# A fused attention and two-layer FFN kernel on one Trainium2 core: attention begun after 11 of 36 bias groups, with four more changes of order

## The chip, the core and the metric

The kernel runs on one core of a Trainium2 chip. The metric is the time of one execution in microseconds (us); the kernel before has a median of 1082.48 us over three runs (1082.42 to 1085.07). The engines are called PE (TensorE, with PEld for its weight loads), DVE (VectorE), ACT (ScalarE), POOL (GpSimd) and SP (SyncE, which here only issues DMAs). All program times below are read from one profiled execution.

## What is computed

Attention over 4 batches, 8 heads, 576 positions of 64 values, with a bias that a small net computes from the distance of two positions; then two FFNs over the 2304 tokens. The parts of the reference that matter:

```python
scores = scale * np.matmul(q, k.transpose(0, 1, 3, 2))
x = (psi_rel / psi_i)[..., None]            # from the positions alone
h = np.maximum(x @ w1 + b1, 0.0)            # 32 hidden values per pair of positions
scores = scores + (h @ w2).transpose(2, 0, 1)[None]
attn = np.exp(scores - np.max(scores, axis=-1, keepdims=True))
attn = attn / (np.sum(attn, axis=-1, keepdims=True) + 1e-09)
x = np.matmul(attn, v)                      # then (2304, 512)
...
h = x @ w_in                                # 512 to 2048, then a rational function g(h)
x = g @ w_out
...
h = np.maximum(np.maximum(x @ w1, x @ w2), x @ w3)   # 512 to 768, three times
out = h @ w_out
```

Weights come in as 64-bit floats; q, k, v and the bias net as 32-bit floats.

## The kernel before

**Bias.** The bias depends on neither batch nor on q and k, so it is made once, in 36 groups of 16 query rows: eight groups for each of the query tiles t = 0 to 3 (128 rows) and four for t = 4 (64 rows). For each group, `bias_hidden` makes four hidden blocks of 128 partitions x 576 columns, the first on ACT (L173), three on DVE (L176); `bias_out` multiplies them with the second layer on PE (L185, 16 records a group), evacuates and scales on ACT (L194, three of the 36 on DVE, L192), and stores the group to a DRAM tensor `bias_d[t]` from ACT's DMA queue (L197). When a tile's last group is stored, `bias_load` fetches that tile's bias for the head pairs p = 0 and 1 back through SP's queue (L204, and L210 to L212 for t = 4); for p = 2 and 3 this comes four units before use. `bias_step` makes the hidden blocks of one group and the output of the group before it.

**Attention.** The work is cut into 80 units (batch b, query tile t, head pair p). In batch 0 the pairs 0 and 1 run first, tile by tile (units 0 to 9: two units for each t); the other pairs run their five tiles one after the other, grouped as ts = [0, 1] and [2, 3, 4]. `attn_tick(n)` does, in the order of a list of step names (`A1` for the first ticks, `A2` for the rest): scores of unit n on PE (`sc`, L233, L243), bias, scale and row minimum on DVE (`r0`, `r1`, L258), exponent and row sum on ACT (`e0`, `e1`, L264), the reciprocal of unit n-1's sums (`n`: POOL L269, DVE L270, POOL L272 spreads it to 128 columns, `rb`), the transposes of unit n-2 (`T`: eight L296, one tail block L302, and the spread reciprocals L303, the last two into one PSUM tile `tt`), their evacuations (`v0` on ACT, `v1` on DVE or ACT), attention x V of a whole group ts (`av`, L338), its scaling by the reciprocals and its store (`st`, L344, L346). The groups of two and three units are cut over as many ticks (`CUT2`, `CUT3`). The step `b` calls `bias_step`; in the first list there are four of it.

**Splits.** q and k are each split into a rounded part and a remainder for PE's fast fp32 form. `split_kq` makes this in six pieces for a head pair, all on POOL (L138 to L153).

**Weights.** The 64-bit weights of the first FFN layer (16 blocks) are converted during attention (`early`: ACT L382, DVE L383 and L391, store to DRAM `wi_n`), spread evenly over the units from `WS` to `WE` by `early_pop` (steps `p1`, `p2`). From unit 61 on they are read back and split (`weight_stages`, ACT L407, remainder L408 on the engine that `low_eng` gives).

**Order.** `manual_schedule` makes the named engines follow the order of the program text; the others get their order from a planner. Before, SP alone follows the text until unit 8; from unit 8 to the end of attention SP, PE and DVE do; five drain ticks behind it run with the first FFN steps in the planner's order; after them all five engines follow the text. The 24 first bias groups stand in the text between the pieces of the first two head pairs' splits (`SB`: two behind each piece), ahead of unit 0.

**Buffers.** 35 slots of SBUF of one size (`slot`) hold hidden blocks, bias outputs, bias tiles, q, k, v, their splits and the exponents. PSUM has two `wide` buffers (bias outputs and scores) and four `bank` buffers (transposes, `tt`, attention x V).

Of the kernel before, what the change touches and what calls it, by code (L numbers as in the profile page):

```python
# [17 lines left out]
P = 128  # L18
# [11 lines left out]
KN = {'NSLOT': 35, 'NRAW': 3, 'NRAWX': 2, 'NATT': 4, 'HB': 0, 'NE': 'd', 'FP': 2, 'BL': 4, 'T4': 0, 'LSP': 1, 'KX': 4, 'HT': 'ss', 'EVP': 'da', 'TTP': 'dda', 'NXS': 4, 'EARLY': 0, 'NM0': 8, 'MAN': 2, 'MANF': 3, 'A1': ['b', 'T', 'sc', 'st', 'r0', 'av', 'b', 'b', 'b', 'sq', 'n', 'r1', 'p2', 'v0', 'v1', 'e0', 'e1'], 'A2': ['sc', 'av', 'p1', 'T', 'r1', 'r0', 'n', 'st', 'p2', 'sq', 'e0', 'e1', 'v0', 'v1'], 'LL': 10, 'SL': 4, 'LL0': 9, 'SL0': 4, 'SQ': [2, 1, 1], 'CUT2': 2, 'CUT3': 3, 'WS': 9, 'WE': 70, 'WT': 61, 'XT': 8, 'XA': 3, 'XB': 8, 'F': ['g2a', 'g2d', 'h', 'g1a', 'w', 'g2p', 'g1d', 'g1p', 'y', 'x', 'g3'], 'LOW': 4, 'LOM': 3, 'LOI': 0, 'GHI': 'dve', 'GLO': 'dve', 'BED': 8, 'BE0': 16, 'NU1': 'pool', 'XE': ['act', 'pool'], 'WR': 1, 'YSP': 'act', 'LAG': 2, 'EV1': 'dve', 'XSE': 'act', 'STQ': 'sp', 'PUQ': 'sp', 'NB0': 0, 'HP': 0, 'SB': 2, 'XLA': 3, 'XLB': 6, 'XSA': 11, 'YL': 10, 'YS': 14, 'WLOW': 1}  # L30
# [7 lines left out]
def tile_attention_moe(  # L38
# [90 lines left out]
    def split_kq(b, p):  # L129
# [4 lines left out]
        lo_eng = pool  # L134
        low = slice(64, P)

        def q_hi():
            pool.tensor_scalar(qs, qr[:, :, :512], 1.0, 0.0, ALU.mult, ALU.add)  # L138

        def q_lo(u):  # L140
            lo_eng.tensor_tensor(qs[low, u], qr[low, u, :512], f32(qs[low, u]), ALU.subtract)

        def k_hi(u):
            pool.tensor_scalar(ks[u][:, 0], kr[:, u], 1.0, 0.0, ALU.mult, ALU.add)

        def k_lo(u):
            pool.tensor_tensor(ks[u][:, 1], kr[:, u], f32(ks[u][:, 0]), ALU.subtract)
# [13 lines left out]
    hid = {}  # L161

    def bias_hidden(t, g):
        hs = []
        for c in range(4):
# [14 lines left out]
    def bias_out(t, g):  # L180
# [106 lines left out]
    def transposes(b, t, p):  # L287
# [315 lines left out]
    bnext = [0]  # L603

    def bias_step():
        i = bnext[0]
        if i < len(bgroups):
            if i == 0:
                bias_hidden(*bgroups[0])
            if i + 1 < len(bgroups):  # L610
                bias_hidden(*bgroups[i + 1])
            t, g = bgroups[i]
# [28 lines left out]
    load_kq(0, 1)
    for p in range(2, KN["FP"]):
        if p == 2:
            load_v(0, 2)
        load_kq(0, p)
    for p in range(KN["FP"]):
        for n, f_ in enumerate(split_kq(0, p)):
            if p >= 2 and KN["LSP"]:
                sqq.append(f_)
            else:  # L650
# [63 lines left out]
    def attn_tick(n):  # L714
# [72 lines left out]
    for n in range(KN["NM0"]):  # L787
        attn_tick(n)
# [101 lines left out]
```

## Time and profile before

| | us |
|---|---|
| median of three runs | 1082.48 (1082.42 to 1085.07) |
| the profiled execution | 1085.02 |
| its span, first to last instruction | 1083.2 |
| PE busy | 1034.7 (96%) |
| DVE busy | 657.7 (61%) |
| ACT busy | 622.8 (57%) |
| POOL busy | 452.7 (42%) |

Engines work side by side, so their busy times don't add up. The stages by the timeline of PE: bias alone from 6 to 59 us, bias and attention to about 88, attention to about 363, the first FFN to about 780, the second to the end. The profile's page cuts the span into 40 equal slices of 27 us; a digit there is the busy share in tenths. In a timeline, each line has the start, the duration, engine, source line, operation, output<-input, shape and count; the bracket behind it is the time in which the engine sat idle before, and what ended it.

### The profile page before, as it was taken

To read this page: it belongs to the slowest core of one execution; us is meant where nothing else is said; L and a number is where in the kernel's file an instruction comes from. 1 tells how busy PE (TensorE), PEld (TensorE's weight loads), DVE (VectorE), ACT (ScalarE), POOL (GpSimd) and SP (SyncE) were. 2 spreads that over 40 slices of the span, in tenths; PEclk is the share of its full clock that TensorE was granted. 3 is DMA by queue.
4 is the path that set the end of the run, shared out by engine and by line. 5 is a ranking of instruction groups with operands and counts; after the bars stand their busy time and mean duration, and the time that the engine had idled before them with its cause. 6 is when DMAs were issued, how large, how long until landed. Compare 5 with 4: busy or idle time off the path is not lost. (4 is left out here: it accounts for less than half of the span.)

```text
span 1083.2 us, 16519 instructions
## 1 busy us (share of the span) xinstructions
PE 1034.7 (96%) x5996; PEld 814.2 (75%) x5996; DVE 657.7 (61%) x1296; ACT 622.8 (57%) x1226; POOL 452.7 (42%) x569
## 2 busy tenths in 40 slices
PE   5689899999998889999999999999999999999998
PEld 2247777777765668878889888788888888888887
DVE  8485667676665789777779877799954211111111
ACT  5685676776776878676678766788733211211111
POOL 7605767677696534332233322333533330211111
PEclk9799999999998889999999999999999999999999
DMA  7486854454453442010020200034243200201010
GB/s 266 138 298 216 294 182 151 158 190 158 157 184 123 147 142 78 1 59 1 0 79 1 79 1 0 24 114 136 84 142 105 78 1 1 78 1 59 1 40 20
DMA packets 43394, 107.94 MB, mean 100 GB/s; under 512 B 4784, under 2 KB 11184, under 8 KB 43312
## 3 DMA queue, kind: packets, MB, share of 16 engines
q1 hardware_dynamic: 38128, 96.27, 26.8%
q10 hardware_dynamic: 5184, 10.62, 2.5%
q8 instruction: 47, 0.77, 0.3%
q14 instruction: 35, 0.29, 0.1%
HBM read 77.90 MB, written 28.97 MB: 99 GB/s over the span
## 5 line engine op out<-in xcount | busy, mean ns | idle before, releaser
L454 PE MATMUL p<-ys,wm 128*128 128x512 f32 (+1 forms) x1080 | 227.0, 368 | 0.0
L454 PE MATMUL ph<-xs,wwi 128*128 128x512 f32 (+1 forms) x960 | 215.9, 373 | 3.5 <-ACT at L743 2.6
L454 PEld LDWEIGHTS p<-ys,wm 128*128 128x128 f32 x1080 | 188.9, 188 | 34.3
L454 PE MATMUL y<-gs,wwo 128*128 128x512 f32 (+1 forms) x905 | 204.4, 373 | 1.3 <-POOL gs L502 1.1
L454 PEld LDWEIGHTS ph<-xs,wwi 128*128 128x128 f32 x960 | 169.7, 190 | 38.4 <-POOL xs L446 3.0
L502 POOL TENSOR_TENSOR gs<-g,gs 128x512 fp32r<-128x512 f32 (+1 forms) x80 | 96.1, 1201 | 237.2 <-ACT gs L501 170.2
L454 PEld LDWEIGHTS y<-gs,wwo 128*128 128x128 f32 x905 | 158.4, 188 | 34.5 <-POOL gs L502 2.4
L264 ACT ACTIVATE e<-e,st 128x576 f32<-128x576 f32 x144 | 111.1, 772 | 61.2 <-DVE st L258 44.3
L258 DVE CUSTOM_DVE_ANT_0 e<-s,bias 128x576 f32<-128x576 f32 x144 | 104.3, 754 | 44.9 <-PE s L233 32.4
L546 POOL TENSOR_TENSOR h2s<-mx,h2s 128x512 fp32r<-128x512 f32 (+1 forms) x30 | 35.5, 1183 | 225.5 <-ACT h2s L545 225.5
L542 DVE TENSOR_TENSOR mx<-p,mx 128x512 f32<-128x512 f32 (+1 forms) x30 | 19.1, 637 | 141.4 <-PE p L454 137.5
L475 ACT ACTIVATE s<-ph,keep 128x512 f32<-128x512 f32 (+1 forms) x80 | 49.5, 618 | 90.3 <-PE ph L454 89.9
L545 ACT CAST h2s<-mx 128x512 fp32r<-128x512 f32 (+1 forms) x30 | 17.3, 578 | 127.8 <-DVE mx L543 127.8
L296 PEld LDWEIGHTS tp<-ident,e 128*128 128x128 f32 x576 | 62.1, 141 | 35.7 <-issue 20.1
L233 PE MATMUL s<-k,qs 128*128 128x288 f32 x512 | 86.4, 309 | 2.2 <-ACT bo L194 1.5
L296 PE MATMUL tp<-ident,e 128*128 128x128 f32 x576 | 81.5, 281 | 1.2 <-ACT at L743 1.2
L477 DVE SCALAR_TENSOR_TENSOR g<-g,keep,s 128x512 f32<-128x512 f32 (+1 forms) x80 | 55.3, 692 | 41.5 <-ACT g L476 40.4
L338 PE MATMUL av<-at,v 128*64 128x320 f32 (+3 forms) x576 | 79.0, 396 | 0.0
L560 PE MATMUL o<-wmo,h2s 128*128 128x512 f32 x324 | 78.6, 390 | 0.0
L233 PEld LDWEIGHTS s<-k,qs 128*128 128x128 f32 x512 | 71.3, 191 | 5.6 <-issue 2.6
L185 PE MATMUL pb<-h,keep 128*32 128x288 f32 x576 | 49.2, 450 | 24.1 <-ACT h L173 23.2
L560 PEld LDWEIGHTS o<-wmo,h2s 128*128 128x128 f32 x324 | 60.4, 188 | 12.6 <-POOL h2s L546 0.4
(98 smaller groups left out, 1599.6 us busy)
## 6 DMA issues: line engine op xcount, KB each, us to landing
bias_d<-bo ACTq DMA_DIRECT2D x36, 288.0 KB, 3.1
kr<-in_k SPq DMA_DIRECT2D x16, 576.0 KB, 4.3
qr<-in_q SPq DMA_DIRECT2D x16, 576.0 KB, 4.3
bias<-bias_d SPq DMA_DIRECT2D x16, 576.0 KB, 5.5
wrm<-in_m SPq DMA_DIRECT2D x18, 512.0 KB, 3.6
wrwin<-in_wi SPq DMA_DIRECT2D x16, 512.0 KB, 5.4
wrwo<-in_wo SPq DMA_DIRECT2D x16, 512.0 KB, 3.6
v<-in_v SPq DMA_DIRECT2D x8, 576.0 KB, 4.3
```

Source lines behind the costliest of these rows:

```text
L185: pe.matmul(pb[32 * c:32 * c + 32, x, :HS], lhsT=hw_sb, rhs=hs[c][:, x * HS:(x + 1) * HS], start=True, stop=True,)
L233: pe.matmul(pt[:, x, :HS], lhsT=qs[:, u, t * P:(t + 1) * P], rhs=ks[u][:, w, x * HS:(x + 1) * HS], start=w == 0, stop=w == 1,)
L258: dve.tensor_tensor_reduce(out=dst, in0=src, in1=bs, op0=ALU.add, op1=ALU.min, scale=-0.125, scalar=3.0e38, accum_out=st[:, u:u + 1],)
L264: act.activation(et[:, u], et[:, u], AF.Exp, bias=st[:, u:u + 1], scale=-1.0, accum_out=st[:, 2 + u:3 + u])
L296: pe.transpose(tp[:, j * P:(j + 1) * P], flat[:, 640 * u + j * P:640 * u + (j + 1) * P], ident)
L338: pe.matmul(po[r, :n], lhsT=l, rhs=m, start=j == 0, stop=j == 4, skip_group_check=True)
L454: pe.matmul(po, lhsT=wpart(key, a, k), rhs=rhs, start=first and i == 0, stop=last and i == 2)
L475: act.activation(s, ph, AF.Abs, scale=B0)
L477: dve.scalar_tensor_tensor(q, q, B1, s, ALU.mult, ALU.add)
L502: pool.tensor_tensor(t[1], u, f32(t[0]), ALU.subtract)
L546: pool.tensor_tensor(t[:, 1], m, f32(t[:, 0]), ALU.subtract)
L560: pe.matmul(po, lhsT=h[:, a, tt * P:(tt + 1) * P], rhs=w[c], start=j == 0 and i == 0, stop=j == NF2 - 1 and i == 2,)
```

## The change

- `KN`: the first list of steps `A1` now holds for 7 ticks, with four hidden steps `h` and four output steps `o` of the bias, two of each ahead of `sc`. `NG0` = 11 groups stand ahead of unit 0. `WS` goes from 9 to 20. `LOI` goes from 0 to 2 (`low_eng`: the remainder of every second block of the first FFN weight on DVE). `CUT2` and `CUT3` are gone.
- The splits of the pairs 0 and 1 are made on DVE, five pieces of each between the groups 2 to 10; their sixth pieces come in the first ticks.
- `bias_hidden` puts a second block on ACT for the groups in `H2` (five of the first eleven); `bias_out` always evacuates on ACT and stores from SP's queue. For t = 0 it also copies the group's rows from slot to slot into the bias tiles of the pairs 0 and 1 (four small DMAs a group), and the load from DRAM is gone for these.
- The reciprocals of unit n-3 are transposed in tick n right behind `sc` (`rb`), into the same `tt` as unit n-2's tail block, and evacuated by DVE in a step of their own (`rv`); the tail block's half is evacuated alone. This needs one drain tick more behind the last unit's transposes.
- Attention x V of a group runs as one piece in one tick.
- The first eleven groups and ticks 0 to 6 follow the text on all five engines. Drain ticks: three instead of five.

The diff, without the parts that only move code:

```diff
-KN = {... 'NM0': 8, ... 'A1': ['b', 'T', 'sc', 'st', 'r0', 'av', 'b', 'b', 'b', 'sq', 'n', 'r1', 'p2', 'v0', 'v1', 'e0', 'e1'], 'A2': ['sc', 'av', 'p1', 'T', 'r1', 'r0', 'n', 'st', 'p2', 'sq', 'e0', 'e1', 'v0', 'v1'], ... 'CUT2': 2, 'CUT3': 3, 'WS': 9, ... 'LOI': 0, ...}
+KN = {... 'NM0': 7, ... 'H2': [2, 4, 6, 8, 10], 'SP0': [2, 6], 'NG0': 11, 'A1': ['h', 'o', 'h', 'o', 'sc', 'rb', 'rv', 'T', 'r0', 'r1', 'h', 'e0', 'e1', 'o', 'v0', 'n', 'h', 'o', 'v1', 'av', 'st', 'sq', 'p2'], 'A2': ['sc', 'rb', 'r0', 'rv', 'av', 'p1', 'T', 'r1', 'n', 'st', 'p2', 'sq', 'e0', 'e1', 'v0', 'v1'], ... 'WS': 20, ... 'LOI': 2, ...}
...
-    def split_kq(b, p):
+    def split_kq(b, p, eng=pool):
...
-            pool.tensor_scalar(qs, qr[:, :, :512], 1.0, 0.0, ALU.mult, ALU.add)
+            eng.tensor_scalar(qs, qr[:, :, :512], 1.0, 0.0, ALU.mult, ALU.add)
...
-            if c == 0:
+            if c == 0 or c == 1 and 8 * t + g in KN["H2"]:
                 act.activation(dst, src, AF.Relu, bias=bcol)
             else:
-                on_pool = c == 3 and KN["HP"] and g % KN["HP"] == 0 and (t, g) >= (1, 4)
-                (pool if on_pool else dve).tensor_scalar(dst, src, bcol, 0.0, ALU.add, ALU.max)
+                dve.tensor_scalar(dst, src, bcol, 0.0, ALU.add, ALU.max)
...
-        if g % KN["BED"] == 1 and 8 * t + g >= KN["BE0"]:
-            dve.tensor_scalar(bo, pb[:, :, :HS], sc, None, ALU.mult)
-        else:
-            act.activation(bo, pb[:, :, :HS], AF.Copy, scale=sc)
-        rows = bias_d[t][g * 16:(g + 1) * 16].rearrange("i h j -> (i h) j")
+        act.activation(bo, pb[:, :, :HS], AF.Copy, scale=sc)
         bo = bo.rearrange("p x j -> p (x j)")
-        act.dma_start(rows, bo)
-
-    bias = {}
+        rows = slice(g * 16, g * 16 + 16)
+        sp.dma_start(bias_d[t][rows].rearrange("i h j -> (i h) j"), bo)
+        if t == 0:
+            for p in range(KN["FP"]):
+                if g == 0:
+                    bt = slot(f"bias{t}_{p}", [P, 2, S], F32)
+                    bias[t, p] = [bt[:, 0], bt[:, 1]]
+                    btile[p] = bt
+                for u in range(2):
+                    sp.dma_start(btile[p][rows, u], bo[2 * p + u::H])
...
-        tt = bank(f"tt{b}_{t}_{p}")
         pe.transpose(tt[:, :P], flat[:, 512:640], ident)
+        evac.append(rows(b, t, p, 0, tt[:, :P]))
+        return evac
+
+    def rows(b, t, p, w, tr):
+        _, a2, off = at[b, t, p]
+        if t < 4:
+            return [(a2[:, w, off:off + P], tr)]
+        return [(a2[r, w, off:off + 64], tr[r, r]) for r in (slice(0, 64), slice(64, P))]
+
+
+    def transpose_sum(b, t, p, tt):
         pe.transpose(tt[:, P:2 * P], rbs.pop((b, t, p)).rearrange("p u d -> p (u d)"), ident)
-        tr = tt[:, :2 * P].rearrange("p (w i) -> p w i", w=2)
-        if t < 4:
-            evac.append((a2[:, :, off:off + P], tr))
-        else:
-            for u in range(2):
-                r = slice(64 * u, 64 * u + 64)
-                evac.append((a2[r, :, off:off + 64], tr[r, :, r]))
-        return evac
...
+    def bias_h():
+        if bnext[0] < len(bgroups):
+            bias_hidden(*bgroups[bnext[0]])
+            bnext[0] += 1
+
+    def bias_o():
...
+                    if t > 0 and not late(t, p):
                         bias_load(t, p)
...
+    with ordered(3):
+        pieces = {}
+        for p in range(2):
+            for n, f_ in enumerate(split_kq(0, p, dve)):
+                if n < 5:
+                    pieces.setdefault(KN["SP0"][p] + n, []).append(f_)
+                else:
+                    sqq.append(f_)
+        bias_h()
+        for i in range(KN["NG0"]):
+            bias_h()
+            for f_ in pieces.get(i, []):
                 f_()
-                for _ in range(KN["SB"] if p < 2 else 0):
-                    bias_step()
+            bias_o()
...
+        u3 = units[n - KN["LAG"] - 1] if KN["LAG"] < n <= NU + KN["LAG"] else None
...
+            elif step == "rb" and (u2 or u3):
+                tt = bank(f"tt{n}")
+                if u3:
+                    sums = transpose_sum(u3[0], u3[2], u3[3], tt)
+            elif step == "rv" and u3:
+                for e_ in sums:
+                    evac("d", e_)
             elif step == "T" and u2:
-                ev = transposes(u2[0], u2[2], u2[3])
+                ev = transposes(u2[0], u2[2], u2[3], tt)
...
-                evac(KN["TTP"][n % len(KN["TTP"])], ev[-1])
-            elif step == "b":
-                bias_step()
+                for e_ in ev[-1]:
+                    evac(KN["TTP"][n % len(KN["TTP"])], e_)
+            elif step == "h":
+                bias_h()
+            elif step == "o":
+                bias_o()
...
-                    av = (u2[0], u2[1], u2[3])
-                    cuts = {1: (5,), 2: (3, 2), 3: (2, 2, 1)}
-                    cut = {1: (5,), 2: cuts[KN["CUT2"]], 3: cuts[KN["CUT3"]]}[len(u2[1])]
-                    avq.extend((av, range(sum(cut[:k]), sum(cut[:k + 1]))) for k in range(len(cut)))
+                    avq.append(((u2[0], u2[1], u2[3]), range(5)))
...
-    for n in range(KN["NM0"]):
-        attn_tick(n)
+    with ordered(3):
+        for n in range(KN["NM0"]):
+            attn_tick(n)
-    while avq or stq or n < NU + KN['LAG']:
+    while avq or stq or n <= NU + KN['LAG']:
```

## Rows read from the trace of the kernel before

**Rows 1.** The page's 40 equal slices: PE's busy share in tenths.
```profile
PE   5689899999998889999999999999999999999998
```

**Rows 2.** Windows view: stretch, length, busy us of PE, PEld, DVE, ACT, POOL, clock, DMA.
```profile
sum 110.00, PE 82.49 PEld 45.83 DVE 75.21 ACT 68.92 POOL 54.27; mean PE 16.50 PEld 9.17 DVE 15.04 ACT 13.78 POOL 10.85
...
310.00:330.00 20.00, 15.32 (x115) 11.35 (x112) 11.03 (x32) 14.00 (x35) 18.28 (x29) 0.95 0.53 165
200.00:300.00 100.00, 99.98 (x738) 74.33 (x737) 69.74 (x195) 72.28 (x170) 70.84 (x129) 1.00 0.51 169
```

**Rows 3.** Timelines of the start, all engines; the last line is POOL's, later.
```profile
5.55 21.98 DVE L176 TENSOR_SCALAR h<-tab_sb,psi 128x576 f32<-128x576 f32 x51
...
9.96 18.47 POOL L138 TENSOR_SCALAR qs<-qr 128x1024 fp32r<-128x1024 f32 x1 [6.89 <-DMA qr<-in_q]
...
34.23 0.74 ACT L194 ACTIVATE bo<-pb,keep 128x576 f32<-128x576 f32 x1 [12.99 <-POOL qtail L153]
...
35.68 6.91 PE L185 MATMUL pb<-h,keep 128*32 128x288 f32 x64 [13.21 <-ACT h L173]
...
92.37 1.05 POOL L138 TENSOR_SCALAR qs<-qr 128x1024 fp32r<-128x1024 f32 x1
```

**Rows 4.** PE's timeline: first scores of units 0, 1, 3 and 10; one bias group.
```profile
58.85 0.80 PE L233 MATMUL s<-k,qs 128*128 128x288 f32 x4
...
61.11 1.18 PE L185 MATMUL pb<-h,keep 128*32 128x288 f32 x16
...
67.08 0.80 PE L233 MATMUL s<-k,qs 128*128 128x288 f32 x4
...
87.41 0.79 PE L233 MATMUL s<-k,qs 128*128 128x288 f32 x4
...
110.01 1.31 PE L233 MATMUL s<-k,qs 128*128 128x288 f32 x8
```

**Rows 5.** Line view: L408 (min/median/max ns, first and last start); small evacuations (busy us, mean ns).
```profile
L408 POOL TENSOR_TENSOR wwi<-wrwi,wwi x15: 1265/1280/1470, 298.4 to 358.2; 128x512 fp32r<-128x512 f32 x15
...
L408 DVE TENSOR_TENSOR wm<-wrm,wm x6: 681/1008/1799, 725.2 to 828.6; 128x512 fp32r<-128x512 f32 x6
L408 DVE TENSOR_TENSOR wwo<-wrwo,wwo x4: 679/680/685, 371.4 to 437.7; 128x512 fp32r<-128x512 f32 x4
...
L317 DVE COPY att<-tt 64x128 f32<-64x128 f32 x19 | 5.5, 288 | 7.6 <-ACT att L315 5.0 <-PE tt L303 2.0
```

**Rows 6.** DMA issues (KB each, us to landing); SP's queue's own waits, 0 to 120 us.
```profile
bias_d<-bo ACTq DMA_DIRECT2D x36, 288.0 KB, 3.1
...
bias<-bias_d SPq DMA_DIRECT2D x16, 576.0 KB, 5.5
...
SPq L204 <- DMA bias_d<-bo: 65.0, 10, 15.2
```

**Rows 7.** Waits for the reciprocals: summed from 100 to 320 us; the longest, in PE's timeline.
```profile
PE tt L303 <- POOL rb L272: 3.2, 2, 1.6
...
329.71 0.48 PE L303 MATMUL tt<-ident,rb 128*128 128x128 f32 x1 [4.68 <-POOL rb L272]
329.84 2.27 PE L233 MATMUL s<-k,qs 128*128 128x288 f32 x8
```

**Rows 8.** One unit of the steady stage: PE's timeline; then VectorE's, a reciprocal and a reduction.
```profile
254.52 1.29 PE L233 MATMUL s<-k,qs 128*128 128x288 f32 x8
255.75 1.30 PE L338 MATMUL av<-at,v 128*64 128x320 f32 x8
256.97 1.09 PE L296 MATMUL tp<-ident,e 128*128 128x128 f32 x8
...
258.04 1.41 PE L233 MATMUL s<-k,qs 128*128 128x288 f32 x8
...
251.79 0.16 DVE L270 RECIPROCAL st<-st 128x1 f32<-128x1 f32 x1 [1.25 <-POOL st L269]
...
252.84 0.76 DVE L258 CUSTOM_DVE_ANT_0 e<-s,bias 128x576 f32<-128x576 f32 x1 [0.30 <-PE s L233]
```

More of the change, by code (lines that the diff above doesn't have):

```diff
@@ L29 @@
 TW = 1148
[L30 removed]
+KN = {'NSLOT': 35, 'NRAW': 3, 'NRAWX': 2, 'NATT': 4, 'HB': 0, 'NE': 'd', 'FP': 2, 'BL': 4, 'T4': 0, 'LSP': 1, 'KX': 4, 'HT': 'ss', 'EVP': 'da', 'TTP': 'dda', 'NXS': 4, 'EARLY': 0, 'NM0': 7, 'MAN': 2, 'MANF': 3, 'H2': [2, 4, 6, 8, 10], 'SP0': [2, 6], 'NG0': 11, 'A1': ['h', 'o', 'h', 'o', 'sc', 'rb', 'rv', 'T', 'r0', 'r1', 'h', 'e0', 'e1', 'o', 'v0', 'n', 'h', 'o', 'v1', 'av', 'st', 'sq', 'p2'], 'A2': ['sc', 'rb', 'r0', 'rv', 'av', 'p1', 'T', 'r1', 'n', 'st', 'p2', 'sq', 'e0', 'e1', 'v0', 'v1'], 'LL': 10, 'SL': 4, 'LL0': 9, 'SL0': 4, 'SQ': [2, 1, 1], 'WS': 20, 'WE': 70, 'WT': 61, 'XT': 8, 'XA': 3, 'XB': 8, 'F': ['g2a', 'g2d', 'h', 'g1a', 'w', 'g2p', 'g1d', 'g1p', 'y', 'x', 'g3'], 'LOW': 4, 'LOM': 3, 'LOI': 2, 'GHI': 'dve', 'GLO': 'dve', 'BED': 8, 'BE0': 16, 'NU1': 'pool', 'XE': ['act', 'pool'], 'WR': 1, 'YSP': 'act', 'LAG': 2, 'EV1': 'dve', 'XSE': 'act', 'STQ': 'sp', 'PUQ': 'sp', 'NB0': 0, 'HP': 0, 'SB': 2, 'XLA': 3, 'XLB': 6, 'XSA': 11, 'YL': 10, 'YS': 14, 'WLOW': 1}
 REBIAS = 2.0 ** -112
@@ L133, in split_kq @@
         kq[b, p] = ks, qs
-        lo_eng = pool
         low = slice(64, P)
         def q_hi():
-            pool.tensor_scalar(qs, qr[:, :, :512], 1.0, 0.0, ALU.mult, ALU.add)
+            eng.tensor_scalar(qs, qr[:, :, :512], 1.0, 0.0, ALU.mult, ALU.add)
         def q_lo(u):
-            lo_eng.tensor_tensor(qs[low, u], qr[low, u, :512], f32(qs[low, u]), ALU.subtract)
+            eng.tensor_tensor(qs[low, u], qr[low, u, :512], f32(qs[low, u]), ALU.subtract)
         def k_hi(u):
-            pool.tensor_scalar(ks[u][:, 0], kr[:, u], 1.0, 0.0, ALU.mult, ALU.add)
+            eng.tensor_scalar(ks[u][:, 0], kr[:, u], 1.0, 0.0, ALU.mult, ALU.add)
         def k_lo(u):
-            pool.tensor_tensor(ks[u][:, 1], kr[:, u], f32(ks[u][:, 0]), ALU.subtract)
+            eng.tensor_tensor(ks[u][:, 1], kr[:, u], f32(ks[u][:, 0]), ALU.subtract)
         def tail(u):
@@ L161, in tile_attention_moe @@
     hid = {}
+    bias, btile = {}, {}
     def bias_hidden(t, g):
@@ L285, in at_tiles, with transposes @@
             at[b, t, p] = a, a2, n * P
-    def transposes(b, t, p):
+    def transposes(b, t, p, tt):
         et, st = ex.pop((b, t, p))
@@ L300, in transposes @@
                 evac.append((a[:, :, :, off:off + 64], tp.rearrange("p (j u i) -> p j u i", j=4, u=2)))
-        tt = bank(f"tt{b}_{t}_{p}")
         pe.transpose(tt[:, :P], flat[:, 512:640], ident)
-        pe.transpose(tt[:, P:2 * P], rbs.pop((b, t, p)).rearrange("p u d -> p (u d)"), ident)
-        tr = tt[:, :2 * P].rearrange("p (w i) -> p w i", w=2)
-        if t < 4:
-            evac.append((a2[:, :, off:off + P], tr))
-        else:
-            for u in range(2):
-                r = slice(64 * u, 64 * u + 64)
-                evac.append((a2[r, :, off:off + 64], tr[r, :, r]))
-        return evac
+        evac.append(rows(b, t, p, 0, tt[:, :P]))
[6 more added lines that the diff above has]
+    def transpose_sum(b, t, p, tt):
+        pe.transpose(tt[:, P:2 * P], rbs.pop((b, t, p)).rearrange("p u d -> p (u d)"), ident)
+        return rows(b, t, p, 1, tt[:, P:2 * P])
     def evac(e, pair):
@@ L602, in tile_attention_moe @@
     bgroups = [(t, g) for t in ((4, 0, 1, 2, 3) if KN["T4"] else range(5)) for g in range(8 if t < 4 else 4)]
[L603 to L612, printed above, removed]
+    bnext = [0, 0]
+    def bias_h():
[3 more added lines that the diff above has]
+    def bias_o():
+        if bnext[1] < len(bgroups):
+            t, g = bgroups[bnext[1]]
             bias_out(t, g)
@@ L615, in bias_step @@
                 for p in range(NP):
-                    if not late(t, p):
+                    if t > 0 and not late(t, p):
                         bias_load(t, p)
-            bnext[0] += 1
+            bnext[1] += 1
     slim = {"wi": wi, "wo": wo}
@@ L636, in wo_todo, with ordered @@
         return src, "wo", f, f < 11, low_eng(KN['LOW'], f)
+    def ordered(m):
+        names = ["SP", "PE", "DVE", "Pool", "Activation"][:(1, 2, 3, 5)[m]]
+        return tc.manual_schedule(engines={getattr(mybir.EngineType, e) for e in names})
     sqq = []
     load_kq(0, 0)
+    load_kq(0, 1)
     load_v(0, 0)
[L641 to L650, printed above, removed]
-                f_()
-                for _ in range(KN["SB"] if p < 2 else 0):
-                    bias_step()
+    with ordered(3):
[10 more added lines that the diff above has]
+            for f_ in pieces.get(i, []):
+                f_()
+            bias_o()
     NB = len(blocks)
@@ L781, in attn_tick @@
                     split_x("x", 0, kc)
-    def ordered(m):
-        names = ["SP", "PE", "DVE", "Pool", "Activation"][:(1, 2, 3, 5)[m]]
-        return tc.manual_schedule(engines={getattr(mybir.EngineType, e) for e in names})
-    for n in range(KN["NM0"]):
-        attn_tick(n)
+    with ordered(3):
+        for n in range(KN["NM0"]):
+            attn_tick(n)
     with ordered(KN["MAN"]):
```

## The prediction

> **What bounds the kernel now.** I read the page's slices first. TensorE (PE) is busy 9 tenths or more in nearly all of them; the rest is 5, 6 and 8 tenths in the first three and 8 tenths in slices 13 to 15, the end of attention [rows 1]. So time can be won only at these two places, and work added to another engine costs only where PE then waits for it. The windows view prices the start: the first 110 us hold 82.5 us of PE [rows 2].
>
> The timelines say why. GpSimd's rounding of the first Q (L138) lasts 18.47 us, from 9.96 to 28.43, while VectorE runs 51 hidden-layer instructions back to back until 27.5; the same instruction takes 1.05 us later on. ScalarE's bias output then waits 12.99 us for a slot that GpSimd's split still holds, and PE 13.21 us for ScalarE [rows 3]. The first scores start at 58.85; unit 10, the first of the steady stage, starts at 110.01 [rows 4]. From there PE is full (99.98 of 100 us between 200 and 300 [rows 2]), but for waits on the softmax reciprocals' transpose [rows 7].
>
> **Start.** Before its first scores the change has 13 bias groups out and 14 hidden layers made. Those are 14 x 3 VectorE instructions, less five that go to ScalarE: 37. At 21.98/51 = 0.43 us [rows 3] that is 15.9 us. The splits of two head pairs lie on VectorE too. No row shows them there; the nearest give: Q rounding 0.43 x 1024/576 = 0.77 (GpSimd's 1.05 is the other end); two K roundings 0.86; two K remainders at 0.68 x 576/512 = 0.77 each, from the two-input form of 512 columns [rows 5]; two Q remainders 0.68 each. That is 4.5 us a pair, 9.0 us in all. Their Q has landed at 9.96, when GpSimd starts on it [rows 3]; VectorE comes to it after 11 hidden instructions, at 5.55 + 4.7 = 10.3, so it doesn't wait. First scores: 5.55 + 15.9 + 9.0, about 31 us.
>
> Then come ticks with four groups and one unit. Before, the first took 8.2 us from scores to scores, the next two 20.3 together [rows 4]. I take 8.2 for the first, 10.2 for the next four, 8.5 for the sixth (one group fewer ahead of its scores): 88.5. From unit 3 to unit 10 the kernel now takes 22.6/7 = 3.23 us a unit [rows 4]; four of these put unit 10 at 101.4, a gain of 8.6. One bound: if PE never waits after 31 us, its 82.5 us of work [rows 2], less 13 groups at 1.18 done by then [rows 4] and less the 2.2 that 64 matmul records lost to the slow clock (6.91 [rows 3] instead of 4 x 1.18), end at 31 + 65.0 = 96.0, a gain of 14. The other: each of the four later query tiles waits for its bias. A tile's last group is out one tick before its first use; store (3.1) and load (5.5) [rows 6], two issues and the evacuation make some 10 us of a tick of 10.2. One more store landing on each costs 4 x 3.1 = 12.4, so the start could even lose 3.8.
>
> The stores on SyncE are 36 of bias and, for tile 0, whose bias is now copied between slots, 32 small ones. What they are moved behind matters: the loads of a bias tile wait for its last store, and hold all later stores and the loads of Q, K and V. Before, this queue waited 65.0 us on bias stores in ten waits [rows 6], with only loads behind them. Now the output slots would come free late, and ScalarE would wait for them. I add nothing to the sum for this; its price is the upper bound above. The Trainium skill (DMA: Bandwidth & Descriptors, Issuing engines are not separate DMA queues) says that another issuing engine only saves issue time. By that alone the move is worth nothing either way and the bound falls away; the queue's own waits in this trace speak against leaving it out.
>
> **Sum order.** The reciprocals' transpose moves from behind a unit's other transposes to behind the next scores. PE waited for it 3.2 us in two waits and 4.68 in a third, after which scores took 2.27 us instead of 1.29 and the slow clock lasted for the attention x V behind them, an estimated 2 in all [rows 7, 8]: some 10 us. The slack won is one unit's scores, 1.23 us [rows 8], so by itself 3.7. But the long wait is GpSimd's backlog (18.28 of 20 us busy from 310 to 330 [rows 2]), and half of the 16 remainders of the first FFN weight, 1.28 us each there [rows 5], go to VectorE. I take 8, between 3.7 and 10. The price: one evacuation becomes two half as wide (0.29 us at that width [rows 5]), one always on VectorE: about 0.2 us a unit there, at most 0.29.
>
> **Attention x V uncut.** The total is the same, but it falls on two units of five instead of on all. A unit without it costs PE 1.23 (scores to attention x V) and 1.07 (transposes to scores), 2.30 us instead of 3.52 [rows 8]. VectorE needs 2 x 0.76 for the reductions, 0.08 for the end of the reciprocal, some 0.3 for its half of the evacuations and 0.4 for the two small ones: 2.3, no less. With a step of weight conversion (0.7 us; 32 of them in 50 units instead of 61) it needs 3.0, and PE waits up to 0.7. If 3 in 5 steps fall on such units: 32 x 0.6 x 0.7 = 13 us at most, and nothing if the two score buffers take it up. I take 4: at most two such units follow each other.
>
> **The rest.** Eight weight remainders on VectorE (0.68 to 1.80 us each [rows 5]) in units 62 to 80, where it idles 9 of 20 us [rows 2]: +1; if that cover is gone, 8. Conversion from unit 20 frees the first units of some 8 steps and makes nothing late: it still ends at unit 70, and block f is read at unit 61 + f or later. Three drain units instead of five, in slices that hold 8 tenths [rows 1]: the planner's order there can change either way, 0 within -4 and +4.
>
> **Sum.** -8.6 - 8 + 4 + 1 = -11.6 us. Against the profiled execution's own 1085.0 (span 1083.2) that is 1073.4. That execution lies 2.5 above the median, 1082.5; against the median it is 1071, which I give.
>
> **Rivals.** (a) The ticks pack densely and nothing is lost later: -14 - 10 + 1, so 1059. For it: the old ticks were in a planner's order, the new are written out. Against: score and bias tiles share two wide buffers. (b) The bias round trip eats the start: +3.8 - 8 + 4 + 1, so 1083. (c) Slower: PE starves in the two neighbouring units without attention x V. VectorE's reciprocal waits there for GpSimd, 1.25 us in one instance [rows 8], and all behind it in VectorE's queue waits too; 2 x (0.7 + 1.25) x 14 rounds is 55 us at worst, half of that in place of the 4 gives 1094. It turns the sign from 15.6 us, 1.1 a round. Against: two score buffers let VectorE lag by some 0.6. (d) The sum order only moves its wait: -3.7 instead of -8, so 1075. (e) VectorE's weight remainders wait for GpSimd's instructions. Beside a busy GpSimd one took 1.80 instead of 0.68 [rows 5]; at 1.80 plus one GpSimd remainder of 1.28, eight of them delay VectorE by 25 us, half of it where it would idle: 1082. The Trainium skill (SBUF — State Buffer, Who interferes with whom) states such a rule: a VectorE instruction with two SBUF inputs and a GpSimd one that reads SBUF exclude each other, and the later one fully blocks. The spread from 0.68 to 1.80 agrees with it, as do the 18.47 us. (f) Attention doesn't start early: slots run out and the 13 us wait comes back in the new order: 1080.
>
> **How the numbers follow.** Forecast 42%, (a) 17, (b) 10, (c) 8, (d) 15, (e) 5, (f) 3. About 0.3%, 3.2 us, is what a measurement of this kernel can tell from no change. Faster than 1079.3: the forecast, (a), nearly all of (d), part of (b), (e) and (f), 79%. Within 0.3%: 12%. Slower than 1085.7: 9%. The range runs from just below (a) to (b), 1057 to 1083; (c) and the tails of (a) and (b) are left out.
>
> **What would show it.** First scores near 31 us and unit 10 near 101. No GpSimd instruction of 18 us. No PE wait above 1 us for the reciprocals around 300 to 330 us. Units without attention x V near 2.3 us in the steady stage; if they take 3 us with PE waiting for VectorE's reductions, the third term is wrong. Reductions of units 2, 4, 6 or 8 that wait for a bias load would make it (b).

## The result and the profile after

The change made the kernel slower: median 1095.72 us (1093.57 to 1096.19, four runs) against 1083.55 for the kernel before measured beside it (four runs), a ratio of 1.010 with a 95% interval of 1.0081 to 1.0119. The profiled execution of after took 1096.02 (span 1094.1). The forecast was 1071, with a chance of 9% on slower.

Landmarks of PE's timeline (us) say where the 11 us came from. A round is one head pair's five units.

| | before | after | difference |
|---|---|---|---|
| scores of unit 0 begin | 58.85 | 30.13 | -28.7 |
| scores of unit 10 begin | 110.01 | 113.9 | +3.9 |
| scores of unit 79, the last, begin | 356.3 | 367.1 | +10.8 |
| first FFN layer begins | 363.19 | 373.44 | +10.3 |
| its eighth step begins | 412.59 | 423.69 | +11.1 |

The rows behind three of these, before at unit 79, then after at units 6, 10 and 79:

```profile
356.27 1.53 PE L243 MATMUL s<-k,qtail 128*128 128x512 f32 x8
...
92.91 0.79 PE L235 MATMUL s<-k,qs 128*128 128x288 f32 x4
...
113.93 1.31 PE L235 MATMUL s<-k,qs 128*128 128x288 f32 x8
...
367.12 1.54 PE L245 MATMUL s<-k,qtail 128*128 128x512 f32 x8
```

So the start, where 8.6 was to be won, lost 3.9; the steady stage, where 3 were to be won, lost 6.9; the rest changed by 0.3. The page's slices (PE, in tenths) and the windows (columns as in [rows 2]):

```profile
PE   7788999999999889999999999999999999999998
...
sum 110.00, PE 89.01 PEld 48.47 DVE 73.27 ACT 71.92 POOL 24.52; mean PE 44.51 PEld 24.23 DVE 36.63 ACT 35.96 POOL 12.26
...
310.00:330.00 20.00, 18.23 (x132) 13.25 (x130) 16.39 (x45) 14.91 (x35) 13.57 (x19) 1.00 0.55 181
200.00:300.00 100.00, 95.05 (x715) 73.77 (x715) 75.97 (x225) 69.16 (x161) 66.94 (x121) 1.00 0.51 168
```

The slices look better than [rows 1]: 7 7 8 8 instead of 5 6 8 9 at the start, which is the earlier beginning. PE is busy 89.0 of the first 110 us instead of 82.5, though part of that is slow clock, and POOL's 54.3 are down to 24.5. But the 99.98 of 100 between 200 and 300 [rows 2] have become 95.05: a loss in the middle, where nothing had been lost before. The stretch 310 to 330 is better (18.23 instead of 15.32).

**The start.** Timelines of after; first DVE and PE, then SP's queue and the grouped line of the small copies (L201: min/median/max ns).

```profile
10.05 0.69 DVE L137 TENSOR_SCALAR qs<-qr 128x1024 fp32r<-128x1024 f32 x1
...
30.13 1.70 PE L235 MATMUL s<-k,qs 128*128 128x288 f32 x8
...
36.69 0.76 DVE L260 CUSTOM_DVE_ANT_0 e<-s,bias 128x576 f32<-128x576 f32 x1 [6.41 <-DMA bias<-bo]
...
37.51 6.93 PE L184 MATMUL pb<-h,keep 128*32 128x288 f32 x64 [5.67 <-DVE st L260]
...
26.76 2.39 SPq L201 DMA_DIRECT2D bias<-bo  x4
29.25 0.53 SPq L193 DMA_DIRECT2D bias_d<-bo  x1
29.81 3.76 SPq L201 DMA_DIRECT2D bias<-bo  x4
33.67 0.53 SPq L193 DMA_DIRECT2D bias_d<-bo  x1
34.24 2.39 SPq L201 DMA_DIRECT2D bias<-bo  x4
36.73 6.00 SPq L193 DMA_DIRECT2D bias_d<-bo  x7
...
L201 SPq DMA_DIRECT2D bias<-bo x32: 492/587/1957, 10.1 to 36.0; - x32
...
51.49 0.98 SPq L206 DMA_DIRECT2D bias<-bias_d  x2
...
56.13 0.76 DVE L260 CUSTOM_DVE_ANT_0 e<-s,bias 128x576 f32<-128x576 f32 x1 [3.71 <-DMA bias<-bias_d]
```

Until 30.13 all is as forecast. Then the first reduction waits 6.41 us for the copies of the eighth group, which SP issues only from 34.24 on. SP had no time to issue them earlier: one store and four copies take 2.9 to 4.4 us of it, while DVE makes a group's hidden blocks in about 2. PE stands 5.67 us, and its next 64 records run at a granted clock of 0.58 (37.5 to 44.4), close to the lower of its two levels (1.2 GHz). The backlog lasts: seven stores stand behind the copies, the load of the next bias tile behind these, and unit 2 waits 3.71 for it. The end of the backlog is seen at tick 7, on POOL, DVE and PE:

```profile
97.08 0.67 POOL L143 TENSOR_SCALAR k<-kr 128x576 fp32r<-128x576 f32 x1 [5.16 <-DMA bias_d<-bo]
...
100.92 0.17 DVE L272 RECIPROCAL st<-st 128x2 f32<-128x2 f32 x1 [4.42 <-POOL st L271]
...
101.83 0.45 PE L315 MATMUL tt<-ident,rb 128*128 128x128 f32 x1 [3.37 <-DVE at L322]
```

POOL's splitting of the third pair waits for a slot that a late store still holds; POOL's normalising stands behind it, DVE behind that, PE behind DVE.

**The steady stage.** PE's waits from 114 to 365 us, and one round (143.9 to 164.1, 20.2 us instead of about 17.1) on SP, DVE and PE:

```profile
PE s L235 <- DVE st L272: 8.4, 8, 2.5
PE tt L303 <- DVE att L322: 4.5, 8, 1.1
PE tt L315 <- POOL rb L274: 1.4, 2, 1.1
...
149.46 0.39 SPq L124 DMA_DIRECT2D kr<-in_k  x1
154.77 0.33 SPq L126 DMA_DIRECT2D qr<-in_q  x1
155.15 0.90 SPq L379 DMA_DIRECT2D wrwin<-in_wi  x2
...
160.44 0.43 DVE L388 TENSOR_SCALAR wrwin<-wrwin 128x512 int32<-128x512 int32 x1 [5.22 <-DMA wrwin<-in_wi]
...
161.81 0.77 PE L235 MATMUL s<-k,qs 128*128 128x288 f32 x4 [2.54 <-DVE st L272]
```

The waits for the reciprocals are nearly gone (1.4 where [rows 7] had 3.2 and 4.68), and 12.9 us of waits for DVE stand in their place. The largest single one begins with a weight load that SP could issue only at 155.15, behind a load of q that had itself waited; DVE, in written order, stands 5.22 for it.

### The profile page after: what moved, and what is told of

Same layout as the page of the kernel before. It is cut to its first block, busy times and chain, and to the rows that moved or that the text cites. A ratio compares the mean times of both kernels' runs of the same rounds, so it can differ in the third digit from the quotient of the medians.

```text
span 1094.1 us, 16663 instructions
## 1 busy us (share of the span) xinstructions
PE 1043.8 (95%) x5996; PEld 825.1 (75%) x5996; DVE 680.4 (62%) x1409; ACT 627.5 (57%) x1231; POOL 413.7 (38%) x547
## 5 line engine op out<-in xcount | busy, mean ns | idle before, releaser
L260 DVE CUSTOM_DVE_ANT_0 e<-s,bias 128x576 f32<-128x576 f32 x144 | 107.7, 751 | 29.2 <-PE s L245 9.5
L235 PE MATMUL s<-k,qs 128*128 128x288 f32 x512 | 90.2, 312 | 9.8 <-DVE st L272 8.4
L343 PE MATMUL av<-at,v 128*64 128x320 f32 (+3 forms) x576 | 73.4, 396 | 4.1 <-DVE att L322 3.2
L298 PEld LDWEIGHTS tp<-ident,e 128*128 128x128 f32 x576 | 65.7, 143 | 13.5 <-issue 12.8
L184 PE MATMUL pb<-h,keep 128*32 128x288 f32 x576 | 58.3, 447 | 16.2 <-DVE st L260 7.9
```

The source lines that it names most:

```text
L184: pe.matmul(pb[32 * c:32 * c + 32, x, :HS], lhsT=hw_sb, rhs=hs[c][:, x * HS:(x + 1) * HS], start=True, stop=True,)
L235: pe.matmul(pt[:, x, :HS], lhsT=qs[:, u, t * P:(t + 1) * P], rhs=ks[u][:, w, x * HS:(x + 1) * HS], start=w == 0, stop=w == 1,)
L260: dve.tensor_tensor_reduce(out=dst, in0=src, in1=bs, op0=ALU.add, op1=ALU.min, scale=-0.125, scalar=3.0e38, accum_out=st[:, u:u + 1],)
L298: pe.transpose(tp[:, j * P:(j + 1) * P], flat[:, 640 * u + j * P:640 * u + (j + 1) * P], ident)
L343: pe.matmul(po[r, :n], lhsT=l, rhs=m, start=j == 0, stop=j == 4, skip_group_check=True)
```

## The experiments

Ratios are against the kernel before, measured beside each group of experiments (medians 1084.1 to 1084.8). "Unit 10" is the start of its scores; it and every other landmark come from one profiled execution.

**1. The bias stores back on ACT's queue.**

```diff
-        sp.dma_start(bias_d[t][rows].rearrange("i h j -> (i h) j"), bo)
+        act.dma_start(bias_d[t][rows].rearrange("i h j -> (i h) j"), bo)
```

> The changed kernel, with the 36 bias stores back on ScalarE's DMA queue; the 32 small copies stay on SyncE's. Theory A (SyncE's queue is the bound of the start: a copy takes 0.59 us to issue, a store 0.53, so 2.9 us or more a group against some 2 us that VectorE needs for one): the first reduction no longer waits 6.4 us for a copy but 1 to 3, unit 2's no longer 3.7 us for its bias tile, and unit 10 starts at 102 to 107 instead of 113.9; the time is 1084 to 1089 instead of 1095.7. Rival B (the ticks are slow because all five engines follow the written order and share two wide buffers): unit 10 moves by less than 3 us, the time is 1093 or more.

1090.42 us, ratio 1.0050 (1.0031 to 1.0070); first scores 36.4, unit 10 at 111.2. That meets neither expectation whole: unit 10 moved by 2.8 us, as in rival B, and the time fell by 5.3, just short of theory A. ACT's timeline shows why it is no cure:

```profile
25.56 0.33 ACTq L193 DMA_DIRECT2D bias_d<-bo  x1
25.94 1.44 ACT L173 ACTIVATE h<-tab_sb,psi 128x576 f32<-128x576 f32 x2 [0.41 <-ACT bo L190]
```

Each store makes ACT wait for its own evacuation to end and then issue: some 0.75 us a group, 2.3 us a group in all, so ACT bounds the first groups. SP is at the 32 copies from 9.45 to 33.7, 24.2 us, of which the issuing itself takes 19.2. So the queue of the stores is worth 5 us, 2.8 of them before unit 10, but the copies stay.

**2. No copies: tile 0's bias goes through DRAM as the others do.**

```diff
-        if t == 0:
-            for p in range(KN["FP"]):
...
-                for u in range(2):
-                    sp.dma_start(btile[p][rows, u], bo[2 * p + u::H])
...
-                    if t > 0 and not late(t, p):
+                    if not late(t, p):
```

> The changed kernel without the 32 small copies: tile 0's bias goes through DRAM like the other tiles'; all stores stay on SyncE's queue. Theory A (the copies are what this queue can't carry; with the stores on ScalarE's queue instead, ScalarE became the bound): the first reduction starts at 32 to 34 us instead of 36.7, unit 2 waits less than 2 us for its bias, unit 10 starts at 103 to 107 instead of 113.9, the time is 1085 to 1090 instead of 1095.7. Rival B (the written order and the two wide buffers bound the ticks): unit 10 at 111 or later, 1093 or more.

1089.74, ratio 1.0062 (1.0042 to 1.0082). The time is in the range of theory A, unit 10 is not:

```profile
109.67 1.30 PE L227 MATMUL s<-k,qs 128*128 128x288 f32 x8
```

The first reduction runs at 31.95 with no wait for a DMA, but unit 10 begins at 109.7, only 4.3 earlier than in after. The other two stalls of the start are still there: unit 2 waits 4.45 for its bias load, and PE 5.3 at tick 7.

**3. Attention x V cut again, in the changed kernel.**

```diff
-                    avq.append(((u2[0], u2[1], u2[3]), range(5)))
+                    av = (u2[0], u2[1], u2[3])
+                    cut = {1: (5,), 2: (3, 2), 3: (2, 2, 1)}[len(u2[1])]
+                    avq.extend((av, range(sum(cut[:k]), sum(cut[:k + 1]))) for k in range(len(cut)))
```

> The changed kernel, with attention x V cut over the ticks of its group again (3 and 2 blocks, or 2, 2 and 1). Theory C (units without attention x V starve PE: 100 us between 200 and 300 hold 95.05 us of PE): PE is at 99 us or more there, the stage from unit 10 to the last scores shrinks by 7 to 12 us from 253.2, the time is 1084 to 1089. Rival D (the added evacuation of the reciprocals on VectorE is what slows the stage): less than 3 us, 1093 or more.

1094.54, ratio 1.0096 (1.0081 to 1.0112). The window from 200 to 300 is full again, which settles whose its 5 us were:

```profile
200.00:300.00 100.00, 99.58 (x733) 73.45 (x732) 77.84 (x230) 71.51 (x167) 69.53 (x128) 1.00 0.53 177
```

But the median falls by only 1.2, far from theory C's 7 to 12 and no more than the intervals leave open: the round from 146.0 now takes 24.2, with DVE waiting 5.30 for a weight load. The two losses hid each other, as experiments 6 and 7 confirm.

**4. Attention x V uncut, alone, in the kernel before.**

```diff
-                    cuts = {1: (5,), 2: (3, 2), 3: (2, 2, 1)}
-                    cut = {1: (5,), 2: cuts[KN["CUT2"]], 3: cuts[KN["CUT3"]]}[len(u2[1])]
+                    cut = (5,)
```

> The kernel before with one edit, attention x V in one piece. Theory C: its steady stage loses 5 to 12 us, the time is 1088 to 1096 against 1083.5. Rival D: within 3 us of the kernel before.

1091.59, ratio 1.0072 (1.0057 to 1.0087). PE's waits from 110 to 365, and the window:

```profile
PE tt L303 <- POOL rb L272: 15.0, 13, 3.6
...
200.00:300.00 100.00, 92.84 (x692) 71.57 (x690) 66.13 (x186) 67.37 (x157) 67.27 (x122) 1.00 0.48 158
```

Some of the short units don't hide the way from a unit's exponents over POOL, DVE and POOL to its sum's transpose. In the changed kernel such units wait for DVE instead.

**5. The order of the sum, alone, in the kernel before** (with the order of the reductions that goes with it).

```diff
-'A2': ['sc', 'av', 'p1', 'T', 'r1', 'r0', 'n', ...]
+'A2': ['sc', 'rb', 'r0', 'rv', 'av', 'p1', 'T', 'r1', 'n', ...]
...
+            elif step == "rb" and (u2 or u3):
+                tt = bank(f"tt{n}")
+                if u3:
+                    sums = transpose_sum(u3[0], u3[2], u3[3], tt)
```

> The kernel before with one edit, the reciprocals' transpose behind the next scores with an evacuation of its own, and the reductions' order that goes with it. Theory C (the sum order helps by the 8 us that were forecast, the uncut attention x V takes it back): 1073 to 1079. Rival D: VectorE's added evacuation costs more than the waits that go, 1083 to 1090.

1085.46, ratio 1.0014 (1.0001 to 1.0027): nothing won, rival D. PE's waits from 110 to 365:

```profile
PE tt L313 <- POOL rb L272: 2.7, 1, 2.7
PE av L341 <- ACT at L754: 2.5, 1, 2.5
PE tt L313 <- ACT at L754: 1.6, 3, 0.6
```

The 7.8 us for rb are down to 2.7, but 4.1 for ACT's evacuations have come. The two rounds from 298.4 on take 41.1 together instead of 43.2; the three early rounds take 18.1 to 18.6 instead of 17.0 to 17.5.

**6 and 7. Weight conversion from unit 9 again; with that, attention x V cut too.** The second has the diff of experiment 3 as well.

```diff
-KN = {... 'WS': 20, ...}
+KN = {... 'WS': 9, ...}
```

> The changed kernel with weight conversion from unit 9 as before. Theory E (from unit 20 on the first converted block's load is issued behind q, k and x transfers that wait in SyncE's queue, and VectorE, which follows the written order, stands 5.2 us for it): that wait is gone, the five units around 144 to 164 us take 17.5 to 18.5 us instead of 20.2, the time is 1091 to 1094. Rival F (the same wait comes at another block, or the eight steps more in the first units cost as much): 1095 or more.

> The changed kernel with attention x V cut again and conversion from unit 9. Theory C with E (uncut attention x V and the late conversion together make the slow steady stage): five units take 17.1 to 17.5 us all through, the time is 1084 to 1089. Rival D (the reciprocals' own evacuation on VectorE is a cost by itself): 1091 or more.

1091.21, ratio 1.0067 (1.0047 to 1.0088); with the cuts 1087.13, 1.0025 (1.0011 to 1.0040). With unit 9 the round from 145.9 takes 16.7 and no wait for wrwin is left. So the later conversion costs 4.5 us beside uncut attention x V and 7.4 beside cut (1094.54 to 1087.13); the uncut form costs 4.1 beside conversion from unit 9.

**8. Experiments 2, 3 and 6 together.**

> The three edits together: no copies, attention x V cut, conversion from unit 9. If A, C and E hold and add up: unit 10 at 103 to 107, five units in 17.1 to 17.5 us, 1074 to 1081, faster than the kernel before. If they stand for one another: 1084 or more.

1082.36, ratio 0.9981 (0.9965 to 0.9996). That is faster than before, but short of the 1074 to 1081 expected. The stage from unit 10 to unit 79 takes 242.5 instead of 246.3, but unit 10 begins at 110.6: tick 7 still stalls (POOL 7.2 for a slot, DVE 6.7, PE 5.7).

**9. In that kernel, the third pair's splitting two ticks later.**

```diff
-KN = {... 'SL0': 4, ...}
+KN = {... 'SL0': 6, ...}
```

> The kernel of e9_nocopies_cuts_ws9 with one number changed: the splitting of the third pair (q, k on POOL) starts two ticks later, SL0 6 instead of 4. In that kernel's trace POOL stands 7.2 us before k L143 (<-DMA bias_d<-bo, from 86.96 to 94.12): its tile k takes a buffer that a late bias store still holds. POOL's order is not the written one any more from tick 7, but the normalising steps of the units then stand behind it: the DVE's reciprocal waits 6.7 for st L263 and PE 5.7 for the sum's evacuation. Theory (a late store holds POOL, POOL holds the sums, the sums hold PE): with the split later the store has landed, the 5.7 us wait of PE goes, the scores of unit 10 begin at 105 to 107 instead of 110.6, and the time falls by 3 to 5 us, 1077 to 1079. Rival one (POOL is short of time): the 9.6 us of rounding then end after tick 10 begins, the scores of unit 10 wait for k instead, they begin at 109 to 112 and the time stays at 1081 to 1084. Rival two (gained early, given back): unit 10 begins at 106, but the units 10 to 20 run into the next loads and conversions and the time stays within 2 us of 1082.

1078.03, ratio 0.9936 (0.9923 to 0.9950), unit 10 at 108.2. The time is the theory's, the way to it is not: unit 10 comes 2.5 us earlier than in experiment 8 and not at 105 to 107, because the late store has found another victim, and another 2.3 are won between unit 10 and unit 79 (240.2 for 242.5), which wasn't followed. ACT, then PE:

```profile
91.74 0.74 ACT L190 ACTIVATE bo<-pb,keep 128x576 f32<-128x576 f32 x1 [5.67 <-DMA bias_d<-bo]
...
92.53 1.33 PE L227 MATMUL s<-k,qs 128*128 128x288 f32 x4 [4.78 <-ACT bo L190]
...
108.15 1.30 PE L227 MATMUL s<-k,qs 128*128 128x288 f32 x8
```

**10. Conversion from unit 20, alone, in the kernel before.**

```diff
-KN = {... 'WS': 9, ...}
+KN = {... 'WS': 20, ...}
```

> The kernel before with one number changed: the conversion of the FFN weights is spread over units 20 to 70 instead of 9 to 70. Theory (the later start costs wherever it stands: the first load of weights is issued on SP behind stores and loads that wait, and the DVE, in written order, stands for it; and the same work in fewer ticks takes more of each): a wait of the DVE of 3 to 5 us for wrwin<-in_wi near 155, a round of about 20 instead of 17.1, and 1086 to 1088. Rival (the wait is one of the changed kernel alone, whose SP queue is fuller): no such wait, rounds of 17.1, 1083 to 1085, the kernel before. The prediction's own value for this part was at most +1.

1093.91, ratio 1.0081 (1.0067 to 1.0096): more than expected. One number, of which the prediction said that it makes nothing late, costs 9.3 us. SP, then DVE:

```profile
152.65 0.33 SPq L126 DMA_DIRECT2D qr<-in_q  x1
153.03 0.90 SPq L374 DMA_DIRECT2D wrwin<-in_wi  x2
...
157.99 0.43 DVE L383 TENSOR_SCALAR wrwin<-wrwin 128x512 int32<-128x512 int32 x1 [5.13 <-DMA wrwin<-in_wi]
```

It is the wait of the changed kernel, in the same place, without a fuller SP queue: the rival falls. PE waits 4.5 us in one piece behind it. A second part lies near 302 to 324, where a round takes 22.2 instead of 18.9; the waits for rb grow there, but what makes them grow wasn't followed.

**11 and 12. In the kernel of experiment 9: the sum order undone, and LOI 0.** The second is one number; the first is the reverse of experiment 5's diff.

```diff
-KN = {... 'LOI': 2, ...}
+KN = {... 'LOI': 0, ...}
```

> The kernel of e10_split_later with the change of the softmax sum undone: rb is transposed at the end of T of its own unit again, with the last probabilities, and the steps stand in the old order (A2 as before, A1 without rb and rv). It asks what the sum order is worth where the rest of the change has been put right. Theory (the sum order only moves its wait: on the kernel before it cost 1.4 us): without it the rounds of the stage from unit 10 to unit 79 stay at 242.8 us within 3, waits of tt for POOL rb come back with 10 to 20 us in all and waits for DVE st fall by as much, and the time is 1076 to 1080. Rival one (the prediction's own: it takes some 8 us out of the long waits for rb): 1084 to 1087 without it. Rival two (it costs): 1073 to 1076, which would make this the best kernel.

> The kernel of e10_split_later with LOI 0 instead of 2: the remainders of all 16 first-layer weights are subtracted on POOL again, where the change gives every second one to the DVE. Theory (the prediction's: the edit is worth about nothing, at most 1 us either way, since the FFN stage is bound by PE): 1077 to 1079. Rival (from unit 61 on POOL is short, so that 8 more subtractions of about 1.1 us make the late units wait for rb): the rounds near 312 to 348 lengthen by 3 to 8 us and the time is 1081 to 1086.

Without the sum order: 1075.02, ratio 0.9911 (0.9896 to 0.9925), the best kernel of all; rival two holds, the order costs 3.0 us, though the interval touches that of experiment 9. The loss lies at the start: unit 10 begins at 104.7 instead of 108.2, and ticks with four groups take 9.2 us instead of 10.2. From unit 10 to unit 79 the order wins 1.5 (240.2 with it, 241.7 without; the 242.8 of the expectation counts from unit 9), and the two rounds from about 290 on take 37.9 with it and 40.1 without. Without it PE is busy 99.36 of 100 us from 200 to 300, and its waits for rb from 115 to 350 are 3.1 in four, not the 10 to 20 expected. With LOI 0: 1081.51, 0.9975 (0.9962 to 0.9987), 3.5 us lost; here the rival holds, and the round from 313.0 takes 23.1 instead of 19.0. DVE's waits for POOL from 280 to 420, with LOI 0 and then, in the second fence, with 2:

```profile
DVE st L264 <- POOL st L263: 11.8, 7, 4.1
```

```profile
DVE st L264 <- POOL st L263: 5.1, 5, 1.9
```

What the best kernel still loses at the start is the round trip of a bias tile, DVE and then PE:

```profile
100.42 0.76 DVE L252 CUSTOM_DVE_ANT_0 e<-s,bias 128x576 f32<-128x576 f32 x1 [7.48 <-DMA bias<-bias_d]
...
102.67 1.97 PE L290 MATMUL tp<-ident,e 128*128 128x128 f32 x8 [5.00 <-ACT at L743]
...
104.72 1.78 PE L227 MATMUL s<-k,qs 128*128 128x288 f32 x8
```

**13. The copies alone, put into the best kernel** (the reverse of experiment 2's diff).

> The kernel of e12_own_tick_sums with the 32 small copies of tile 0's bias put back on SP. It prices the copies where nothing else of the change is wrong: there the first reduction found its bias without a wait and the scores of unit 10 began at 104.7. Theory (SP's queue is the bound of the start: 32 issues of 0.59 and 11 stores of 0.53 take 24.7 us of it, and the loads of later tiles and keys stand behind them): the first reduction waits some 4 to 6 us for bias<-bo, PE idles as long, later bias stores hold buffers, unit 10 begins at 109 to 112 and the time is 1080 to 1084. Rival (the start had slack for it; the copies cost only together with the later splitting at tick 5): unit 10 at 105 to 107, 1075 to 1078.

1080.41, ratio 0.9964 (0.9952 to 0.9976), unit 10 at 109.5 instead of 104.7: the copies cost 5.4 us, by the wait that they made in the changed kernel:

```profile
36.76 0.76 DVE L260 CUSTOM_DVE_ANT_0 e<-s,bias 128x576 f32<-128x576 f32 x1 [6.28 <-DMA bias<-bo]
```

**14. LOI 2 alone, in the kernel before.**

```diff
-KN = {... 'LOI': 0, ...}
+KN = {... 'LOI': 2, ...}
```

> The kernel before with one number changed: every second of the 16 first-layer weights has its remainder subtracted on the DVE instead of POOL (LOI 2). It asks whether the waits around 300 to 330 belong to this edit or to the sum order, which alone left the wait for rb at 2.7 us and cost 1.4. Theory (those waits are POOL's backlog of remainders, and the edit, not the sum order, takes it away): the wait of 4.68 for rb falls under 1.5, the rounds of 18.9 and 24.3 shorten by 3 to 5 us together, first ph near 359 and 1079 to 1082. Rival one (only the start's earlier end makes it count): 1083 to 1086, the kernel before. Rival two (the DVE's remainders wait beside a busy POOL): over 1087.

1081.92 (1078.94 to 1086.05), ratio 0.9981 (0.9968 to 0.9994): 2.4 us won, with a wide scatter. In the profiled execution (1078.99, 2.9 below the median) the rounds of 18.9 and 24.3 take 17.8 and 19.9, and PE's waits from 280 to 420 for rb are down from 6.3, though the longest, 2.0, is over the 1.5 expected:

```profile
PE tt L303 <- POOL rb L272: 2.5, 2, 2.0
```

## Why the prediction was wrong, step by step

**First scores: right.** 30.13 for 31. DVE's rounding of Q took 0.69 (estimate 0.77), and the 18.47-us instruction is gone.

**Ticks with four groups: right where nothing stalled.** From 74.30 to 84.44 one took 10.14, for 10.2. With the stalls before it, unit 6 began at 92.9 for 88.5.

**Four more units at 3.23: wrong.** From unit 6 to unit 10 after took 21.0 us where the sum has 12.9, which is 8.1 of the 12.5 us by which unit 10 came late (113.9 for 101.4). The mean of units 3 to 10 didn't hold for the last four: before itself took 15.0 for them (95.03 to 110.01), because its units 4 to 6 stood close behind unit 3. With the early start they took 16.7 (experiment 1) to 23.0 (experiment 8), and 21.2 in the best kernel.

**Stores and copies on SP: the step that lost the start.** "I add nothing to the sum for this" gave the 32 small copies, which the prediction names, no time on the queue. At 0.587 each, with eight stores at 0.53, they need 23 us of a queue that has some 20, from the first group's output at 9.69 to the scores at 30.13; they took 26.9, to 36.63, and set the time of the first reduction. The upper bound had priced only one store landing for each of the later tiles; that the start came out at +3.9, beside its +3.8, is by accident. The rate could have been guessed from the trace of before, where the nearest form, a load of strided rows, takes SP as long:

```profile
109.69 0.59 SPq L211 DMA_DIRECT2D bias<-bias_d  x1
```

The Trainium skill (DMA: Bandwidth & Descriptors, Issuing engines are not separate DMA queues) says that the issue time saved by a second issuing engine is usually small beside the DMA itself. For one copy the trace is near that: 0.587 us of issue, and a landing 2.0 us later (medians). For 32 in line it differs: their issues took 20.1 us of SP in after and 19.2 in experiment 1, where no store stood between them, and that, not the landing, was the wait.

With the copies gone and the splitting moved, the start did win, but little: unit 10 at 108.2 instead of 110.0. With the sum order undone too it is 104.7, 5.3 of the 8.6. There PE still loses 5.0 to a bias tile's round trip, the mechanism of rival (b).

**Slots.** Tick 7's chain was in no part of the sum; rival (f) had slots running out, but at the old place. Two ticks' delay of the splitting was worth 4.3 us (experiments 8 and 9).

**Sum order: -8 was wrong in sign.** It cost 1.4 us on the kernel before, hardly clear of nothing, and 3.0 in the corrected one. The term took the waits for rb [rows 7] for the price of the order. In the two rounds around 300 to 330 the order did win 2.1 to 2.3; but waits for ACT's evacuations and longer early rounds (experiment 5) or longer first ticks (experiment 11) took more, rival (d) and beyond it. Most of the gain near 310 to 330 that I put down to it belongs to LOI (5.5 us of two rounds in experiment 14), which I had priced at +1 and which wins 2.4 to 3.5: POOL's backlog was the cause, as the prediction itself said of the long wait, and the edit that lightens POOL is the one that pays. Rival (e)'s blocked remainders didn't come: the eight on DVE in after took 0.68 to 1.23 us, not 1.80 (line view, ns):

```profile
L413 DVE TENSOR_TENSOR wwi<-wrwi,wwi x8: 681/726/1227, 318.7 to 372.6; 128x512 fp32r<-128x512 f32 x8
```

The lock between DVE and POOL that the Trainium skill states (SBUF — State Buffer, Who interferes with whom) may be in that spread; as a price of this edit no run here shows it. The 18.47 us, which the prediction counts for that rule as well, don't fall under it as worded there: the DVE instructions beside that rounding read one tensor and one column each, not two tensors.

**Attention x V uncut: the mechanism was right, the size was not.** +4 with bounds 0 and 13; 7.5 on the kernel before, 4.1 in the changed one. Most short units did run as PE alone would have them: from unit 12 on, 27 of the 40 without attention x V took 2.2 us or less. The other 13 took 2.4 to 5.6; PE stood 12.9 us for DVE from 114 to 365, rival (c)'s mechanism at a fraction of its 55.

**Conversion from unit 20: 0 was wrong.** "Makes nothing late" looked at when the weights are read, not at when the first load is issued. Moved into the steady stage it stands on SP behind a load of q that waits for its buffer, and DVE, in written order, stands behind the load: 9.3 us on the kernel before, 4.5 to 7.4 in the changed one.

**Drain: right.** From unit 79 to the first FFN layer 6.3 instead of 6.9, to its eighth step 50.3 behind that instead of 49.4.

**The sum as measured**, along one path from after (1095.72) to the best kernel (1075.02): cuts back -1.2, conversion from unit 9 -7.4, no copies -4.8, splitting later -4.3, sum order undone -3.0. The medians were taken at different times, between which the kernel before varied from 1083.55 to 1084.78, so the step of 1.2 by itself says nothing. The shares depend on the order of the steps; that each is a loss doesn't, for the uncut form, the conversion, the copies and, only just, the sum order, which were each tried in two settings. What is then left of the change (the earlier start, the stores on SP, LOI 2) is with the later splitting 9.8 us faster than the kernel before.

## What to carry to other kernels

When DMAs are moved or added, count the issues of each group on its queue at a measured duration for that form, and compare the sum with the time in which the group is produced; then name what stands behind them. When work in the background is begun later, ask what its first load will stand behind and who stands behind it in written order, not only when the result is due. And a wait that a profile shows at an instruction isn't the price of that instruction's place in the order: try the edits one by one, since here two of the losses hid each other and a small edit carried most of the gain ascribed to a large one. A mean over several units holds for the last of them only if the trace shows them evenly spaced.

## What the runs showed of the hardware

- In after, the issue of a DMA on SP took different times by form, and for one form too: medians of 0.33 to 0.42 us for x_d stores and for loads of k, q and weights, 0.587 for a copy of 16 rows between slots (0.49 to 1.96), 0.42 for a bias store (0.32 to 0.91; 0.53 between the copies).
- On ACT's queue a store that depends on ACT's own last instruction costs about 0.75 us: 0.41 of idle time and 0.33 of issue (experiment 1).
- After 5.67 us of idling in after, PE ran 6.9 us at a granted clock of 0.58; from 46.3 to 51.1 it was at 1.00 again.
